# A PSUM free list, whole-row weight loads and one joined round in an attention + SwiGLU kernel

## The chip, the cores and the metric

The kernel runs on one core of one Trainium2 chip. The metric is the device time of one execution in microseconds (us). TensorE does matrix products into PSUM, which both kernels use as eight banks of 128 x 512 FP32 values; VectorE and ScalarE carry results out of PSUM; GpSimd issues the loads that cast to bf16; SyncE issues stores and DMA transposes.

## The reference, cut to what matters

```python
a = softmax(phi, axis=2)                    # over the 576 positions; 8 batches, 8 heads, 32 memories
k_m = einsum('bhsm,bhsd->bhmd', a, k)       # "K sums"
v_m = einsum('bhsm,bhsd->bhmd', a, v)       # "V sums"
attn = softmax(q @ k_m.T / sqrt(64), axis=-1)
x = (attn @ v_m) as rows of 512             # 4608 tokens
g, val = x @ w_gate, x @ w_val              # 512 -> 1536
out = (silu(g) * val) @ w_out               # 1536 -> 512
```

The kernel never forms `x`. For each batch it forms U = v_m @ W (a "U round", one per chunk of 512 columns of `w_gate` and `w_val`), and then the gates and values as `attn @ U`.

Of the kernel before, what the change touches and what calls it, by code (L numbers as in the profile page):

```python
# [14 lines left out]
def kernel(  # L15
# [39 lines left out]
    work = ctx.enter_context(tc.tile_pool(name="work", bufs=3))  # L55
    ps = ctx.enter_context(tc.tile_pool(name="ps", bufs=6, space=bass.MemoryType.PSUM))
    po = ctx.enter_context(tc.tile_pool(name="po", bufs=2, space=bass.MemoryType.PSUM))

# [5 lines left out]
    phis, kvs, qs, qTs = {}, {}, {}, {}  # L64
    box = {}
    Q_SLOT = (0, 1, 0, 0, 1, 0, 1, 0)

# [48 lines left out]

    def load_w(which, c, half):

        src = (moe_w_gate, moe_w_val)[which]
        if half == 0:  # L120
            W[which, c] = wpool.tile(
                [128, 2, NP, HC], BF16, tag=f"W{which}{c}", name=f"W{which}{c}"
            )
        f0 = c * CH + half * HC
        nc.gpsimd.dma_start(
            out=W[which, c][:, half],
            in_=src[:, f0:f0 + HC].rearrange("(i p) f -> p i f", p=128),
        )

    WO = {}  # L130
# [107 lines left out]
    def kv_T(b, parts):  # L238
        p = ps.tile([128, 3, 128], BF16, tag="b", name="p_T")
        if 0 in parts:  # L240
            kTs[b] = att.tile([128, 3, 128], BF16, tag="kT", name="t_kT")
        if 1 in parts:
            nc.tensor.transpose(p[:, 2], bvs.pop(b).rearrange("p g d -> p (g d)"), ident)
        if 0 in parts:
            bk = bks.pop(b)
            for g in range(NG):
                nc.tensor.transpose(p[:, g], bk[:, g].rearrange("p a d -> p (a d)"), ident)
        lo, hi = (0 if 0 in parts else 2), (3 if 1 in parts else 2)
        nc.vector.tensor_copy(out=kTs[b][:, lo:hi], in_=p[:, lo:hi])

    def kv_items(b, beside=None):


        def run_sums():
            o = NG * 2 * D
            p = ps.tile([128, o + NG], FP32, tag="b", name="p_kv")
            kv_denominators(b, p, o)
            kv_sum(b, p, (0, 1))
            kv_reciprocal(b, p, o)
            kvv = p[:, 0:o].rearrange("p (g w d) -> p g w d", g=NG, w=2)  # L260
            k_norm(b, kvv[:, :, 0:1, :])
            v_norm(b, kvv[:, :, 1, :])
            if beside:
                beside()

        return [run_sums, lambda: kv_T(b, (0, 1))]

    def k_items(b):


        def denominators():
            p = ps.tile([128, NG], FP32, tag="b", name="p_S")
            kv_denominators(b, p, 0)
            kv_reciprocal(b, p, 0)

        def sums():
            p = ps.tile([128, NG * D], FP32, tag="b", name="p_kv")
            kv_sum(b, p, (0,))
            k_norm(b, p.rearrange("p (g a d) -> p g a d", g=NG, a=1))

        return [denominators, sums, lambda: kv_T(b, (0,))]

    def v_direct(b):


        p = ps.tile([128, NP, M], FP32, tag="b", name="p_vT")
        for i in range(NP):
            for j in range(J):
                for g in range(NG):
                    nc.tensor.matmul(  # L290
                        p[64 * g:64 * g + 64, i],
                        lhsT=kvs[b][:, 1, 2 * i + g, j * D:(j + 1) * D],
                        rhs=ephis[b][:, j, g, i],
                        start=(j == 0),
                        stop=(j == J - 1),
                        tile_position=(0, 64 * g),
                    )
        nc.vector.tensor_copy(out=kTs[b][:, 2], in_=p.rearrange("p i m -> p (i m)"))
        scaled.add(b)

    def q_T(b, g, n, eng="v"):


        pq = ps.tile([128, 2, HALF], BF16, tag="b", name="p_q")
        for i in range(2):
# [13 lines left out]
        else:  # L319
            nc.vector.tensor_copy(out=t, in_=pq)  # L320

    def gv_banks():
        return [
            ps.tile([128, CH], FP32, tag="b", name=f"p_{'gv'[r]}") for r in range(2)
        ]

    def scores(b, g):
# [12 lines left out]
        for r in range(2):  # L340
            nc.scalar.activation(out=e[:, r], in_=p[r][:, 0:HALF], func=AF.Exp, scale=sm_scale)  # L341
        es[b, g] = e

    lzs = {}

    def z_inv(b, g):
# [3 lines left out]
        for r in range(2):  # L350
            nc.tensor.matmul(  # L351
                p[r][:, 0:HALF], lhsT=bones, rhs=es[b, g][:, r], start=True, stop=True
            )
            nc.scalar.activation(out=lz[:, r], in_=p[r][:, 0:HALF], func=AF.Ln)
        nc.scalar.activation(out=lz, in_=lz, func=AF.Exp, scale=-1.0)  # L355
        lzs[b, g] = lz
# [10 lines left out]

    def u_round(b, parts, evac, spare=-1):


        banks = []
        for n_part, (which, c, halves) in enumerate(parts):
            pool, tag = (po, "o") if n_part == spare else (ps, "b")
            w0, w1, h0, h1 = which[0], which[-1] + 1, halves[0], halves[-1] + 1
            n = (h1 - h0) * HC
            p = [
                pool.tile([128, 2, HC], FP32, tag=tag, name=f"p_u{g}").rearrange(
                    "p a f -> p (a f)"
                )
                for g in range(NG)  # L380
            ]
            for w in which:
                o = (w - w0) * n
                for i in range(NP):
                    for g in range(NG):
                        nc.tensor.matmul(  # L386
                            p[g][32 * i:32 * i + 32, o:o + n],
                            lhsT=kTs[b][64 * g:64 * g + 64, 2, 32 * i:32 * i + 32],
                            rhs=W[w, c][64 * g:64 * g + 64, h0:h1, i],
                            start=True,  # L390
# [3 lines left out]
            for g in range(NG):  # L394
# [6 lines left out]
                src = p[g][:, 0:(w1 - w0) * n].rearrange("p (a f) -> p a f", f=HC)  # L401
                banks.append((dst, src, rSs[b][:, g, 0] if b in scaled else None))
        for (t, p, r), e in zip(banks, evac):
            if e == "a":
# [6 lines left out]
            else:  # L411
                nc.vector.tensor_scalar(out=t, in0=p, scalar1=r, scalar2=None, op0=ALU.mult)


# [7 lines left out]
    def gv_half(b, s, which):  # L422

        jf, r = s // 2, s % 2
        c, o = jf // 4, jf % 4
        p = ps.tile([128, CH], FP32, tag="b", name=f"p_{'gv'[which]}")
        for g in range(NG):
# [6 lines left out]
            )  # L434
        return p[:, 0:HALF]

    def gv_gate(b, s):
# [5 lines left out]
        sg = work.tile([128, HALF], BF16, tag="sg", bufs=8, name="t_sg")  # L443
        nc.scalar.activation(out=sg, in_=gate, func=AF.Silu)  # L444
        col = (b % 2) * S + r * HALF
        dst = hts[b // 2, jf][:, col:col + HALF]

        def mul():
            val = gv_half(b, s, 1)
            nc.vector.tensor_tensor(out=dst, in0=sg, in1=val, op=ALU.mult)  # L450

# [26 lines left out]
    def out_units(c, u, eng):  # L478
# [3 lines left out]
        def unit(jf):  # L482
            def run():
                if jf == 0:
                    mine["p"] = po.tile([128, DM], FP32, tag="o", name="p_oo")
                nc.tensor.matmul(  # L486
# [6 lines left out]
                if jf == NJF - 1:  # L493
# [3 lines left out]
                    else:  # L497
                        nc.vector.tensor_copy(out=t_o, in_=mine["p"])  # L498
                    for (r0, m, bb, jj, pp) in token_segments(2 * c * S + 128 * u, 128):
                        nc.sync.dma_start(  # L500
# [7 lines left out]
    def out_units_end(c, u):  # L508
# [4 lines left out]
        def unit(half, jf):  # L513
            def run():
                if jf == 0:
                    mine["p"] = po.tile([128, h], FP32, tag="o", name="p_oo")
                nc.tensor.matmul(  # L517
# [6 lines left out]
                if jf == NJF - 1:  # L524
                    t_o = work.tile([128, h], FP32, tag="to", name="t_o")
                    nc.scalar.copy(out=t_o, in_=mine["p"])
                    segs = token_segments(2 * c * S + 128 * u, 128)
                    for n, (r0, m, bb, jj, pp) in enumerate(segs):
# [23 lines left out]

    def u_item(b, c, evac="avav", spare=-1):

        return lambda: u_round(b, (((0,), c, (0, 1)), ((1,), c, (0, 1))), evac, spare)

    def u_half(b, which, c, half, evac, spare=-1):

        return lambda: u_round(b, ((which, c, (half,)),), evac, spare)

# [26 lines left out]
    def warm(n):  # L587

        p = po.tile([128, DM], FP32, tag="o", name="p_oo")
        for _ in range(n):  # L590
            nc.tensor.matmul(p[:, 0:128], lhsT=bones, rhs=bones, start=True, stop=True)  # L591


# [17 lines left out]
    load_v(1)  # L611
    for c in range(NCH):
        for half in range(2):
            for which in range(2):
                load_w(which, c, half)
    load_wo(0)
# [51 lines left out]
    for s in range(4):  # L668
        gv_gate(0, s)
    run([u_half(0, (1,), 0, 0, "va"), u_half(1, (1,), 0, 0, "va", 0)])  # L670
    for s in range(2):
        gv_gate(1, s)
    flush_mul(3)
    run([u_half(0, (0, 1), 0, 1, "va", 0)])
    flush_mul(2)
    run(g1[2:4])
    run([u_half(1, (0, 1), 0, 1, "av", 0)] + g0[4:8] + g1[4:5])
    for c in range(1, NCH):
        s = 8 * c
        run([u_item(0, c, spare=1)] + g1[s - 3:s] + g0[s:s + 5])  # L680
        run([u_item(1, c, spare=1)] + g0[s + 5:s + 8] + g1[s:s + 5])
    run(g1[-3:])
# [101 lines left out]
```

## The kernel before: the parts that the change touches

PSUM comes from two pools: six banks rotate through everything, two are kept for output sums, for a short burst of "warm-up" products, and as a spare for some U rounds.

```python
ps = tile_pool(name="ps", bufs=6, space=PSUM)
po = tile_pool(name="po", bufs=2, space=PSUM)
...
def warm(n):                               # keeps TensorE busy until data comes
    p = po.tile([128, DM], FP32, tag="o", name="p_oo")
    for _ in range(n):
        nc.tensor.matmul(p[:, 0:128], lhsT=bones, rhs=bones, start=True, stop=True)
...
for c in range(NCH):                       # three chunks, two halves, gate and value
    for half in range(2):
        for which in range(2):
            load_w(which, c, half)         # 128 x 4 x 256, cast to bf16 by GpSimd's queue
...
run([u_half(0, (0, 1), 0, 1, "va", 0)])    # U round: batch 0, second half of chunk 0
flush_mul(2)
run(g1[2:4])                               # two gate/value slots of batch 1
run([u_half(1, (0, 1), 0, 1, "av", 0)] + g0[4:8] + g1[4:5])
for c in range(1, NCH):                    # chunks 1 and 2 of batches 0 and 1
    s = 8 * c
    run([u_item(0, c, spare=1)] + g1[s - 3:s] + g0[s:s + 5])
    run([u_item(1, c, spare=1)] + g0[s + 5:s + 8] + g1[s:s + 5])
```

A slot is one gate (two products of 288 columns, then SiLU on ScalarE) and one value (two products, then a multiplication on VectorE). In the trace these are `p_g`, `p_v`, `t_sg` and `t_h`; a U round is `p_u` into `t_U`; output sums are `p_oo`. From batch 2 on, slots are mixed with output products of the batches before, and one U round and the K/V sums of the next batch lie in between.

The softmax here doesn't subtract the row's maximum and nothing guards it: scores larger than these inputs give would overflow.

## Time and profile before

| | before |
|---|---|
| median of the timed runs | 249.0 us (248.97 to 249.04) |
| span in the profile | 247.4 us |
| first gate starts | 27.98 us |
| last matmul starts | 243.32 us, 215.34 us after the first gate |

Read it from TensorE: its busy share is 97%, but a share hides short holes. I measured holes as the distance between two starts less the pace of a steady stream (216 ns for 512 columns, 122 ns for 288). The lines are in the prediction; there the columns of a timeline row are start, duration, engine, line, operation, tiles and count, and in brackets an idle time with what ended it.

### The profile page before, as it was taken

Reading aid. Unit: us, or ns where it says so; the run is one execution under the profiler, and the core shown is the slowest. Engines: PE = TensorE matmul, PEld = TensorE weight load, DVE = VectorE, ACT = ScalarE, POOL = GpSimd, SP = SyncE. Lnnn points to the kernel's source line nnn. Section 1 sums busy time; section 2 is a strip of 40 time slices with the busy share of each in tenths; the row PEclk is TensorE's granted clock in tenths of the full one; section 3 lists DMA queues with packets and bytes.
Section 4 is the critical chain, followed back from the end, with each engine's and each line's share of the span. In section 5 each row is a group of like instructions: output and inputs, shape, how many; then the busy total and the mean of one; then the engine's idle time right before and its main releaser. Section 6 shows DMA issues by size and latency. Waiting matters only on the chain.

```text
span 247.4 us, 6614 instructions
## 1 busy us (share of the span) xinstructions
PE 239.5 (97%) x2600; PEld 150.7 (61%) x2600; DVE 158.5 (64%) x337; ACT 165.0 (67%) x356; POOL 54.5 (22%) x85
## 2 busy tenths in 40 slices
PE   7998899999999999999999999999999999999993
PEld 7966567774544765467645665476646655467543
DVE  0146499993437688479847778478846876587420
ACT  2467789885087568966896677966895677676201
POOL 8342455000060004070505240090007000000000
PEclk9999999999999999999999999999999999999999
DMA  7999999999689986997897599589414411310143
GB/s 183 205 203 203 196 198 200 233 197 199 126 160 244 236 186 89 212 283 139 122 239 204 90 119 235 166 119 197 91 48 116 72 42 42 87 42 0 45 128 85
DMA packets 49167, 37.00 MB, mean 150 GB/s; under 512 B 15984, under 2 KB 43888, under 8 KB 49136
## 3 DMA queue, kind: packets, MB, share of 16 engines
q0 software_dynamic: 27632, 22.42, 57.5%
q1 hardware_dynamic: 20496, 13.37, 22.9%
q10 hardware_dynamic: 1008, 0.79, 1.2%
q8 instruction: 20, 0.33, 0.5%
q14 instruction: 11, 0.09, 0.1%
HBM read 42.47 MB, written 9.44 MB: 210 GB/s over the span
## 4 chain that ended last, share of the span: by engine, by line
PE 75%; DMA 20%; POOL 3%; issue 1%; ACT 0%; POOLq 0%
PE p_oo L486 32%; PE p_g L428 17%; PE p_v L428 17%; DMA t_kv<-in_v_dram 14%; PE p_u L386 4%; DMA W<-in_moe_w_val_dram 4%; DMA t_qT<-t_q 2%; PE p_kv L183 2%; PE p_oo L517 1%; POOL t_q L93 1%; POOL t_kv L81 1%; PE p_g L351 0%; PE p_v L351 0%; PE p_g L331 0%; POOL t_q L100 0%
## 5 line engine op out<-in xcount | busy, mean ns | idle before, releaser
L486 PE MATMUL p_oo<-WO,t_h 128*128 128x512 bf16 x420 | 108.6, 379 | 0.0
L444 ACT ACTIVATE t_sg<-p_g 128x288 bf16<-128x288 f32 x192 | 76.6, 413 | 31.3 <-PE p_g L428 24.2
L450 DVE TENSOR_TENSOR t_h<-t_sg,p_v 128x288 bf16<-128x288 bf16 x192 | 83.9, 453 | 18.0 <-PE p_v L428 14.1
L428 PEld LDWEIGHTS <-t_U 128*128 128x128 bf16 x768 | 74.2, 98 | 30.7 <-issue 2.5
L428 PE MATMUL p_g<-t_A,t_U 128*128 128x288 bf16 x384 | 77.5, 286 | 0.0
L428 PE MATMUL p_v<-t_A,t_U 128*128 128x288 bf16 x384 | 76.9, 286 | 0.0
L486 PEld LDWEIGHTS <-t_h 128*128 128x128 bf16 x420 | 39.5, 98 | 41.1 <-issue 6.0
L498 DVE COPY t_o<-p_oo 128x512 f32<-128x512 f32 x27 | 18.6, 691 | 32.1 <-PE p_oo L486 29.4
L410 DVE CAST t_U<-p_u 128x512 bf16<-128x512 f32 x42 | 26.7, 684 | 6.8 <-PE p_u L386 6.8
L406 ACT CAST t_U<-p_u 128x512 bf16<-128x512 f32 x30 | 15.8, 592 | 9.0 <-PE p_u L386 9.0
L496 ACT COPY t_o<-p_oo 128x512 f32<-128x512 f32 x8 | 4.7, 588 | 20.5 <-PE p_oo L486 10.6
L100 POOL DMA_DIRECT2D t_q<-in_q_dram x6 | 4.7, 782 | 60.6 <-DMA t_qT<-t_q 59.8
L591 PE MATMUL p_oo<-bones 128*128 128x128 bf16 x198 | 14.6, 234 | 1.5 <-DVE bones L606 1.5
L386 PE MATMUL p_u<-W,t_kT 64*32 64x512 bf16 (+1 forms) x416 | 15.6, 365 | 0.5 <-DMA W<-in_moe_w_val_dram 0.3
L153 ACT ACTIVATE t_ephi<-t_phi 96x768 bf16<-96x768 f32 x16 | 12.5, 843 | 4.3 <-DMA t_phi<-in_phi_dram 4.2
L591 PEld LDWEIGHTS <-bones 128*128 128x128 bf16 x198 | 12.8, 106 | 2.2 <-DVE bones L606 1.5
L166 POOL COPY t_mark<-t_A 1x1 bf16<-1x1 bf16 x4 | 0.7, 182 | 53.9 <-DVE t_A L360 53.9
L360 DVE TENSOR_TENSOR t_A<-t_E,t_lz 128x576 bf16<-128x576 bf16 x16 | 11.5, 750 | 0.3 <-ACT t_lz L355 0.3
L355 ACT ACTIVATE t_lz<-t_lz 128x576 f32<-128x576 f32 x16 | 10.9, 684 | 0.5
L341 ACT ACTIVATE t_E<-p_g 128x288 bf16<-128x288 f32 x16 | 6.6, 412 | 6.9 <-PE p_v L331 6.3
L170 POOL TENSOR_TENSOR t_es<-t_es,t_ephi 96x256 f32<-96x256 f32 x16 | 10.7, 668 | 1.3
L408 ACT ACTIVATE t_U<-p_u,t_rS 128x512 bf16<-128x512 f32 (+1 forms) x14 | 8.3, 628 | 2.9 <-PE p_u L386 2.9
(58 smaller groups left out, 164.1 us busy)
## 6 DMA issues: line engine op xcount, KB each, us to landing
t_kv<-in_k_dram POOLq DMA_DIRECT2D x8, 576.0 KB, 9.8
t_kv<-in_v_dram POOLq DMA_DIRECT2D x8, 576.0 KB, 14.5
out_dram<-t_o SPq DMA_DIRECT2D x23, 192.0 KB, 2.5
t_phi<-in_phi_dram POOLq DMA_DIRECT2D x6, 576.0 KB, 15.2
t_q<-in_q_dram POOLq DMA_DIRECT2D x6, 576.0 KB, 7.4
out_dram<-t_o SPq DMA_DIRECT2D x24, 128.0 KB, 2.4
W<-in_moe_w_gate_dram POOLq DMA_DIRECT2D x6, 256.0 KB, 13.2
W<-in_moe_w_val_dram POOLq DMA_DIRECT2D x6, 256.0 KB, 12.2
```

The lines of the kernel that those rows point to most:

```text
L153: nc.scalar.activation(out=t[:, :, g].rearrange("p j i m -> p i j m"), in_=src[:, g], func=AF.Exp)
L355: nc.scalar.activation(out=lz, in_=lz, func=AF.Exp, scale=-1.0)
L360: nc.vector.tensor_tensor(out=a, in0=es.pop((b, g)), in1=lzs.pop((b, g)), op=ALU.mult)
L386: nc.tensor.matmul(p[g][32 * i:32 * i + 32, o:o + n], lhsT=kTs[b][64 * g:64 * g + 64, 2, 32 * i:32 * i + 32], rhs=W[w, c][64 * g:64 * g + ...
L406: nc.scalar.copy(out=t, in_=p)
L410: nc.vector.tensor_copy(out=t, in_=p)
L428: nc.tensor.matmul(p[:, 0:HALF], lhsT=Us[b, c, g][:, o // 2, which, 128 * (o % 2):128 * (o % 2 + 1)], rhs=atts[b, g][:, r], start=(g == 0) ...
L444: nc.scalar.activation(out=sg, in_=gate, func=AF.Silu)
L450: nc.vector.tensor_tensor(out=dst, in0=sg, in1=val, op=ALU.mult)
L486: nc.tensor.matmul(mine["p"], lhsT=hts[c, jf][:, 128 * u:128 * (u + 1)], rhs=WO[jf], start=(jf == 0), stop=(jf == NJF - 1),)
L498: nc.vector.tensor_copy(out=t_o, in_=mine["p"])
L591: nc.tensor.matmul(p[:, 0:128], lhsT=bones, rhs=bones, start=True, stop=True)
```

## The change

Its intent: let a bank be taken as soon as it is free, whoever used it; move the weights in fewer and longer pieces; save two switches of TensorE between tile sizes. The core of the diff, with cuts:

```diff
-    ps = ctx.enter_context(tc.tile_pool(name="ps", bufs=6, space=bass.MemoryType.PSUM))
-    po = ctx.enter_context(tc.tile_pool(name="po", bufs=2, space=bass.MemoryType.PSUM))
+    ps = ctx.enter_context(tc.tile_pool(name="ps", bufs=1, space=bass.MemoryType.PSUM))
+    free = [f"B{n}" for n in range(8)]
+    held = {}
+    def bank(shape, dtype, name):
+        tag = free.pop(0)
+        t = ps.tile(shape, dtype, tag=tag, name=name)
+        held[id(t)] = tag, t
+        return t
+    def done(*tiles):
+        for t in tiles:
+            free.append(held.pop(id(t))[0])
 ...   (every ps.tile and po.tile becomes bank(...), with done(...) after its last reader)
     def warm(n):
-        p = po.tile([128, DM], FP32, tag="o", name="p_oo")
+        p = bank([128, DM], FP32, "p_warm")
         for _ in range(n):
             nc.tensor.matmul(p[:, 0:128], lhsT=bones, rhs=bones, start=True, stop=True)
+        free.insert(0, held.pop(id(p))[0])
 ...
+    for c in range(1, NCH):
+        for which in range(2):
+            load_w(which, c)               # 128 x 4 x 512
 ...
-    run([u_half(0, (0, 1), 0, 1, "va", 0)])
+    run([u_half(0, (0, 1), 0, 1, "va"), u_half(1, (0, 1), 0, 1, "av")])
     flush_mul(2)
-    run(g1[2:4])
-    run([u_half(1, (0, 1), 0, 1, "av", 0)] + g0[4:8] + g1[4:5])
+    run(g1[2:4] + g0[4:8] + g1[4:5])
```

More of the change, by code (lines that the diff above doesn't have):

```diff
@@ L115, with load_w, w_part @@
     HC = CH // 2
-    def load_w(which, c, half):
+    def load_w(which, c, half=None):
         src = (moe_w_gate, moe_w_val)[which]
-        if half == 0:
+        split = half is not None
+        if not half:
             W[which, c] = wpool.tile(
-                [128, 2, NP, HC], BF16, tag=f"W{which}{c}", name=f"W{which}{c}"
+                [128, 2, NP, HC] if split else [128, NP, CH], BF16,
+                tag=f"W{which}{c}", name=f"W{which}{c}",
             )
-        f0 = c * CH + half * HC
+        f0, n = (half * HC, HC) if split else (0, CH)
         nc.gpsimd.dma_start(
-            out=W[which, c][:, half],
-            in_=src[:, f0:f0 + HC].rearrange("(i p) f -> p i f", p=128),
-        )
+            out=W[which, c][:, half] if split else W[which, c],
+            in_=src[:, c * CH + f0:c * CH + f0 + n].rearrange("(i p) f -> p i f", p=128),
+        )
+    def w_part(which, c, i, g, halves):
+        w = W[which, c][64 * g:64 * g + 64]
+        h0, h1 = halves[0], halves[-1] + 1
+        return w[:, h0:h1, i] if c == 0 else w[:, i, HC * h0:HC * h1]
     WO = {}
@@ L238, in kv_T @@
     def kv_T(b, parts):
-        p = ps.tile([128, 3, 128], BF16, tag="b", name="p_T")
+        p = bank([128, 3, 128], BF16, "p_T")
         if 0 in parts:
@@ L249, in kv_T @@
         nc.vector.tensor_copy(out=kTs[b][:, lo:hi], in_=p[:, lo:hi])
+        done(p)
     def kv_items(b, beside=None):
@@ L255, in run_sums @@
             o = NG * 2 * D
-            p = ps.tile([128, o + NG], FP32, tag="b", name="p_kv")
+            p = bank([128, o + NG], FP32, "p_kv")
             kv_denominators(b, p, o)
@@ L262, in run_sums @@
             v_norm(b, kvv[:, :, 1, :])
+            done(p)
             if beside:
@@ L271, in denominators @@
         def denominators():
-            p = ps.tile([128, NG], FP32, tag="b", name="p_S")
+            p = bank([128, NG], FP32, "p_S")
             kv_denominators(b, p, 0)
             kv_reciprocal(b, p, 0)
+            done(p)
         def sums():
-            p = ps.tile([128, NG * D], FP32, tag="b", name="p_kv")
+            p = bank([128, NG * D], FP32, "p_kv")
             kv_sum(b, p, (0,))
             k_norm(b, p.rearrange("p (g a d) -> p g a d", g=NG, a=1))
+            done(p)
         return [denominators, sums, lambda: kv_T(b, (0,))]
     def v_direct(b):
-        p = ps.tile([128, NP, M], FP32, tag="b", name="p_vT")
+        p = bank([128, NP, M], FP32, "p_vT")
         for i in range(NP):
@@ L298, in v_direct @@
         nc.vector.tensor_copy(out=kTs[b][:, 2], in_=p.rearrange("p i m -> p (i m)"))
+        done(p)
         scaled.add(b)
     def q_T(b, g, n, eng="v"):
-        pq = ps.tile([128, 2, HALF], BF16, tag="b", name="p_q")
+        pq = bank([128, 2, HALF], BF16, "p_q")
         for i in range(2):
@@ L320, in q_T @@
             nc.vector.tensor_copy(out=t, in_=pq)
+        done(pq)
     def gv_banks():
-        return [
-            ps.tile([128, CH], FP32, tag="b", name=f"p_{'gv'[r]}") for r in range(2)
-        ]
+        return [bank([128, CH], FP32, f"p_{'gv'[r]}") for r in range(2)]
     def scores(b, g):
@@ L341, in scores @@
             nc.scalar.activation(out=e[:, r], in_=p[r][:, 0:HALF], func=AF.Exp, scale=sm_scale)
+        done(*p)
         es[b, g] = e
@@ L354, in z_inv @@
             nc.scalar.activation(out=lz[:, r], in_=p[r][:, 0:HALF], func=AF.Ln)
+        done(*p)
         nc.scalar.activation(out=lz, in_=lz, func=AF.Exp, scale=-1.0)
@@ L366, with u_round @@
     scaled = set()
-    def u_round(b, parts, evac, spare=-1):
+    def u_round(b, parts, evac):
         banks = []
-        for n_part, (which, c, halves) in enumerate(parts):
-            pool, tag = (po, "o") if n_part == spare else (ps, "b")
+        for which, c, halves in parts:
             w0, w1, h0, h1 = which[0], which[-1] + 1, halves[0], halves[-1] + 1
             n = (h1 - h0) * HC
-            p = [
-                pool.tile([128, 2, HC], FP32, tag=tag, name=f"p_u{g}").rearrange(
-                    "p a f -> p (a f)"
-                )
-                for g in range(NG)
-            ]
+            p = [bank([128, CH], FP32, f"p_u{g}") for g in range(NG)]
             for w in which:
@@ L388, in u_round @@
                             lhsT=kTs[b][64 * g:64 * g + 64, 2, 32 * i:32 * i + 32],
-                            rhs=W[w, c][64 * g:64 * g + 64, h0:h1, i],
+                            rhs=w_part(w, c, i, g, halves),
                             start=True,
@@ L401, in u_round @@
                 src = p[g][:, 0:(w1 - w0) * n].rearrange("p (a f) -> p a f", f=HC)
-                banks.append((dst, src, rSs[b][:, g, 0] if b in scaled else None))
-        for (t, p, r), e in zip(banks, evac):
+                banks.append((dst, src, p[g], rSs[b][:, g, 0] if b in scaled else None))
+        for (t, p, home, r), e in zip(banks, evac):
             if e == "a":
@@ L412, in u_round @@
                 nc.vector.tensor_scalar(out=t, in0=p, scalar1=r, scalar2=None, op0=ALU.mult)
+            done(home)
     hts = {}
@@ L425, in gv_half @@
         c, o = jf // 4, jf % 4
-        p = ps.tile([128, CH], FP32, tag="b", name=f"p_{'gv'[which]}")
+        p = bank([128, CH], FP32, f"p_{'gv'[which]}")
         for g in range(NG):
@@ L434, in gv_half @@
             )
-        return p[:, 0:HALF]
+        return p
     def gv_gate(b, s):
@@ L443, in gv_gate @@
         sg = work.tile([128, HALF], BF16, tag="sg", bufs=8, name="t_sg")
-        nc.scalar.activation(out=sg, in_=gate, func=AF.Silu)
+        nc.scalar.activation(out=sg, in_=gate[:, 0:HALF], func=AF.Silu)
+        done(gate)
         col = (b % 2) * S + r * HALF
@@ L449, in mul @@
             val = gv_half(b, s, 1)
-            nc.vector.tensor_tensor(out=dst, in0=sg, in1=val, op=ALU.mult)
+            nc.vector.tensor_tensor(out=dst, in0=sg, in1=val[:, 0:HALF], op=ALU.mult)
+            done(val)
         pend.append(mul)
@@ L484, in run @@
                 if jf == 0:
-                    mine["p"] = po.tile([128, DM], FP32, tag="o", name="p_oo")
+                    mine["p"] = bank([128, DM], FP32, "p_oo")
                 nc.tensor.matmul(
@@ L498, in run @@
                         nc.vector.tensor_copy(out=t_o, in_=mine["p"])
+                    done(mine["p"])
                     for (r0, m, bb, jj, pp) in token_segments(2 * c * S + 128 * u, 128):
@@ L515, in run @@
                 if jf == 0:
-                    mine["p"] = po.tile([128, h], FP32, tag="o", name="p_oo")
+                    mine["p"] = bank([128, h], FP32, "p_oo")
                 nc.tensor.matmul(
@@ L526, in run @@
                     nc.scalar.copy(out=t_o, in_=mine["p"])
+                    done(mine["p"])
                     segs = token_segments(2 * c * S + 128 * u, 128)
@@ L551, in q_items, with u_item, u_half @@
         ]
-    def u_item(b, c, evac="avav", spare=-1):
-        return lambda: u_round(b, (((0,), c, (0, 1)), ((1,), c, (0, 1))), evac, spare)
-    def u_half(b, which, c, half, evac, spare=-1):
-        return lambda: u_round(b, ((which, c, (half,)),), evac, spare)
+    def u_item(b, c, evac="avav"):
+        return lambda: u_round(b, (((0,), c, (0, 1)), ((1,), c, (0, 1))), evac)
+    def u_half(b, which, c, half, evac):
+        return lambda: u_round(b, ((which, c, (half,)),), evac)
     def u_three(b):
@@ L611 @@
     load_v(1)
-    for c in range(NCH):
-        for half in range(2):
-            for which in range(2):
-                load_w(which, c, half)
+    for half in range(2):
+        for which in range(2):
+            load_w(which, 0, half)
+    for c in range(1, NCH):
+        for which in range(2):
+            load_w(which, c)
     load_wo(0)
@@ L669 @@
         gv_gate(0, s)
-    run([u_half(0, (1,), 0, 0, "va"), u_half(1, (1,), 0, 0, "va", 0)])
+    run([u_half(0, (1,), 0, 0, "va"), u_half(1, (1,), 0, 0, "va")])
     for s in range(2):
@@ L673 @@
     flush_mul(3)
-    run([u_half(0, (0, 1), 0, 1, "va", 0)])
+    run([u_half(0, (0, 1), 0, 1, "va"), u_half(1, (0, 1), 0, 1, "av")])
     flush_mul(2)
-    run(g1[2:4])
-    run([u_half(1, (0, 1), 0, 1, "av", 0)] + g0[4:8] + g1[4:5])
+    run(g1[2:4] + g0[4:8] + g1[4:5])
     for c in range(1, NCH):
         s = 8 * c
-        run([u_item(0, c, spare=1)] + g1[s - 3:s] + g0[s:s + 5])
-        run([u_item(1, c, spare=1)] + g0[s + 5:s + 8] + g1[s:s + 5])
+        run([u_item(0, c)] + g1[s - 3:s] + g0[s:s + 5])
+        run([u_item(1, c)] + g0[s + 5:s + 8] + g1[s:s + 5])
     run(g1[-3:])
```

## The prediction

> **What bounds the kernel now.** I read first the page's busy shares, then the waits of TensorE, then the TensorE timeline around each wait, and last the chain that ended last. The page:
>
> ```profile
> span 247.4 us, 6614 instructions
> PE 239.5 (97%) x2600; PEld 150.7 (61%) x2600; DVE 158.5 (64%) x337; ACT 165.0 (67%) x356; POOL 54.5 (22%) x85
> L486 PE MATMUL p_oo<-WO,t_h 128*128 128x512 bf16 x420 | 108.6, 379 | 0.0
> L428 PE MATMUL p_g<-t_A,t_U 128*128 128x288 bf16 x384 | 77.5, 286 | 0.0
> ```
>
> A busy share of 97% does not by itself say that TensorE works at its full rate, so I used distances between starts. In the chain, 28 output matmuls take 6.04 us, which is 216 ns each; in the timeline one pair of 288-column matmuls follows the last by 0.245 us, 122 ns each. Both are the pace of a stream with no hole. From 56 us to the end I found only one hole beyond that pace and the mode changes. So the span can shrink only where TensorE has holes, and those lie before 86 us. Four matter. The waits of TensorE:
>
> ```profile
> PE p_vT L290 <- DMA t_kv<-in_v_dram: 0.9, 1, 0.9
> PE p_u L386 <- DMA W<-in_moe_w_val_dram: 0.3, 1, 0.3
> PE p_u L386 <- DMA W<-in_moe_w_gate_dram: 0.2, 1, 0.2
> ```
>
> The first and third (25.6 and 27.1 us) wait for the last V tile and for the first half of weight chunk 0, and the change leaves both loads as they are. The second is chunk 1 of the value weights; then a small repeated hole, then one for K and V of batch 3 (TensorE timeline, three windows):
>
> ```profile
> 35.36 0.41 PE L428 MATMUL p_v<-t_A,t_U 128*128 128x288 bf16 x2
> 35.70 0.41 PE L386 MATMUL p_u<-W,t_kT 64*32 64x512 bf16 x8
> 36.39 0.41 PE L386 MATMUL p_u<-W,t_kT 64*32 64x512 bf16 x8 [0.29 <-DMA W<-in_moe_w_val_dram]
> ...
> 42.55 0.41 PE L428 MATMUL p_v<-t_A,t_U 128*128 128x288 bf16 x2
> 42.85 0.41 PE L428 MATMUL p_g<-t_A,t_U 128*128 128x288 bf16 x2
> 43.15 0.41 PE L428 MATMUL p_v<-t_A,t_U 128*128 128x288 bf16 x2
> ...
> 85.27 0.44 PE L203 MATMUL p_kv<-ones,t_ephi 96*128 96x1 bf16 x12
> 85.78 0.85 PE L183 MATMUL p_kv<-t_kv,t_ephi 96*32 96x128 bf16 x48
> ```
>
> The value half of the round could start at 35.70 + 0.24 = 35.94 and starts at 36.39: a hole of 0.45 us (the view shows 0.29 because it counts modelled ends). At 42.85 and 43.15 a pair comes after 0.30 instead of 0.245 us: 0.11 us a round, three rounds, 0.33 us. At 85.78 the K/V sums start 0.14 us later than the twelve tiny matmuls before them and the usual 0.09 us change would let them. The chain of waits says why:
>
> ```profile
> 25.86 10.40 DMA W<-in_moe_w_val_dram
> ...
> 63.16 4.98 DMA t_qT<-t_q
> ...
> 70.25 15.49 DMA t_kv<-in_v_dram
> 85.78 0.85 PE p_kv L183 x48
> ```
>
> V of batch 3 lands at 85.74, behind a DMA transpose (63.16 to 68.13) that waited for Q of batch 2, the last of the first 28 GpSimd loads (landed at 63.06). That is one unbroken transfer chain from the start of the kernel.
>
> **What the Trainium skill says.** "Perfetto Trace Analysis", section Matmul Optimizations, advises that all 8 PSUM banks be used; here 6 rotate among everything and 2 are kept for outputs, and the trace shows what that costs: 0.33 us. "DMA: Bandwidth & Descriptors", section Why small descriptors are slow (HBM only), names a fixed cost per packet. The trace agrees in kind only: a 512-byte packet takes 60 ns and a 1024-byte one 98 ns, but what the queue moves hardly changes, as the next view shows. "TensorEngine Tiling (Array Packing)", section Key Properties, says that changing the tiling mode drains TensorE; the trace shows 94 ns on entry to a U round (64x32 tiles) and 92 ns on exit, beyond the pace.
>
> ```profile
> 27.00:39.00 12.00, 11.59 (x155) 7.55 (x156) 9.93 (x23) 10.25 (x25) 6.82 (x9) 1.00 1.45 197
> 41.70:47.00 5.30, 5.30 (x56) 3.66 (x54) 5.19 (x12) 4.73 (x12) 0.78 (x1) 1.00 1.29 204
> ```
>
> The last column is GB/s: 197 while half-chunk weights stream (512-byte packets), 204 while output weights (1024-byte) and K do.
>
> **The change part by part.**
>
> *Whole rows.* Eight GpSimd loads of 256 KB become four of 512 KB, with the same bytes in the same order behind the same loads. Before, landings of 256 KB follow each other by 1.33 us (26.95 to 41.61 us in 11 steps), so 512 KB take 2.67; an output-weight load of 512 KB takes 2.59 or 2.60 (41.61 to 44.20, 47.14 to 49.74). That is 0.07 us a load, 0.14 us for the two of chunk 1 and 0.28 us for all four. The window rates give 2.1 MB x (1/197 - 1/204 GB/s) = 0.37 us; I take 0.30. So chunk 1 lands at about 36.1 instead of 36.26, and everything queued behind chunk 2, Q of batch 2 and so V of batch 3 included, lands about 0.3 us earlier. Four issues fewer at 0.74 us each on GpSimd save nothing: the transfers are queued ahead without a gap.
>
> *Joined rounds.* The instruction lists show 2600 matmuls in both kernels. One exit and one entry go away: 92 + 94 = 0.19 us at 32.8 us. But TensorE then meets the wait for chunk 1 at 36.39, and simply waits 0.19 us longer. On the path: nothing.
>
> *Eight banks in order of release.* In the stretch from 36.4 to 56 us VectorE is as full as TensorE: from one evacuation of U at 41.31 to the next at 46.00, 4.69 us, it never rests, while TensorE needs 4.58 (eight slots of 0.49 and a round of 0.65). TensorE is held at the seventh bank it asks for after a round, at 42.85, because with six rotating banks that is the one of the first new gate, whose SiLU ends just then. With eight in a row, the seventh and eighth are those of the round's second half, free at about 42.5 and 42.7, earlier than asked for (42.79 and 43.04). The lag that VectorE builds up is 0.11 us a round over four rounds, about what the two extra banks hold. So most of the 0.33 us goes: say 0.30.
>
> *Sum.* TensorE gets to 85 us earlier by 0.14 (chunk 1) + 0.30 (banks) = 0.44 us. V of batch 3 comes earlier by 0.3 only. The K/V sums start at the later of the two: before, they started 0.14 us after TensorE was ready, so the gain there is the smaller of 0.44 + 0.14 and 0.3, that is **0.3 us**. The hole at 85.78 grows from 0.14 to about 0.28 us. After it TensorE has no hole, and nothing of the change reaches the rest. 248.98 - 0.3 = **248.7 us**, 0.1%.
>
> **The rivals.**
>
> *The transfer chain gives nothing.* A row piece of 2 KB is read at a pitch of 6 KB, while output weights are read without a gap; the higher rate may belong to those. 512-byte packets already move 197 of 204 GB/s, which speaks for this. Then V lands when it did, and the time is 248.9 to 249.0 although TensorE saved 0.3 us earlier.
>
> *The transfer chain gives more,* for instance because the four larger loads are queued earlier. Against it: the queue had no gap to fill. Then TensorE binds: 0.44 + 0.14 = 0.58 us, 248.4.
>
> *A new wait for a bank.* Outputs, which hold a bank for twelve matmuls, now stand in the same line as gates and values, so a late output copy (ScalarE's waits 9.7 us for a store near 69 us) could hold up a gate. Against it: at most one or two output banks are held, so six or seven remain for the rest, and TensorE had no hole there with six. I allow it 0.3 us of loss: 249.0 to 249.3.
>
> *VectorE stays the bound at 40 to 56 us.* More banks let TensorE run ahead but make VectorE no faster. That matters only if the four rounds outlast the extra banks; even so the result at 85.78 is set by V, and the time would stay at 248.7.
>
> **Range and chances.** Three runs of the kernel before lie within 0.07 us. The sum of the holes that the change can touch is 0.45 + 0.33 + 0.14 + 0.19, about 1.1 us, the most that it could give, and the losses I can name are some 0.3 us. The range is 248.1 to 249.2, with the centre at 248.7. Two per cent would be 5 us: no part has that size, so both outer chances are 0.01.
>
> **What would show it.** Right: no pair after 0.30 us at 42 to 53 us; the last of the chunk-1 weights landing near 36.1; one U round fewer with 64x256 matmuls, and the hole before 36.4 grown to about 0.5 us; V of batch 3 landing near 85.4 and TensorE waiting for it about 0.3 us; from there on the same rows shifted by one constant. Wrong: pairs still 0.30 us apart (the banks were not the cause), V landing at 85.7 (rows do not help), a new wait of TensorE on a copy after 56 us (the single list hurts), or a landing that moves by more than 0.5 us.

## The result, and the profile after

The changed kernel takes 248.6 us in the median of four runs: 248.39, 248.42, 248.78, and one of 252.27; the three fast runs alone have a median of 248.42. Executions over 1.5% slower than the fastest of the same kernel are left out of the means. The kernel before takes 249.0. The ratio of the fast runs is 0.9981, a gain of 0.47 us, with a 95% interval of 0.9961 to 1.0001, so the times alone do not quite exclude that nothing was gained. (A ratio is the mean time of one kernel's fast runs over that of the other's in the same rounds, so not quite the ratio of the medians.) The page of the changed kernel, its busy shares and the shares by engine of the chain that ended last:

```profile
span 246.6 us, 6607 instructions
PE 239.5 (97%) x2600; PEld 151.2 (61%) x2600; DVE 157.9 (64%) x337; ACT 164.5 (67%) x356; POOL 51.4 (21%) x81
...
PE 95%; DVE 1%; ACT 1%; issue 0%
```

The last line is the news. In the kernel before it read:

```profile
PE 75%; DMA 20%; POOL 3%; issue 1%; ACT 0%; POOLq 0%
```

So transfers left the chain altogether, and TensorE now binds from its first instruction. The three windows of TensorE that the prediction showed, in the changed kernel:

```profile
35.54 0.41 PE L452 MATMUL p_v<-t_A,t_U 128*128 128x288 bf16 x2
35.88 0.63 PE L409 MATMUL p_u<-W,t_kT 64*32 64x512 bf16 x16
36.43 0.42 PE L452 MATMUL p_g<-t_A,t_U 128*128 128x288 bf16 x2
...
42.49 0.41 PE L452 MATMUL p_g<-t_A,t_U 128*128 128x288 bf16 x2
42.74 0.41 PE L452 MATMUL p_v<-t_A,t_U 128*128 128x288 bf16 x2
42.98 0.41 PE L452 MATMUL p_g<-t_A,t_U 128*128 128x288 bf16 x2
...
84.65 0.44 PE L226 MATMUL p_kv<-ones,t_ephi 96*128 96x1 bf16 x12
85.03 0.85 PE L206 MATMUL p_kv<-t_kv,t_ephi 96*32 96x128 bf16 x48
```

All three holes are gone: the round on chunk 1 runs in one piece, the pairs follow each other by 0.245 us, and the K/V sums start 0.38 us after the tiny matmuls, where the kernel before needed 0.51. From there on every row is 0.75 us earlier. (Chunk 1 landed at 35.81 us, just before TensorE came for it at 35.88.) But the start of TensorE is not earlier, it is later. Before and after:

```profile
25.62 0.94 PE L290 MATMUL p_vT<-t_ephi,t_kv 96*64 96x32 bf16 x48 [0.90 <-DMA t_kv<-in_v_dram]
26.49 0.40 PE L591 MATMUL p_oo<-bones 128*128 128x128 bf16 x4
27.08 0.41 PE L386 MATMUL p_u<-W,t_kT 64*32 64x256 bf16 x16 [0.20 <-DMA W<-in_moe_w_gate_dram]
```

```profile
25.98 0.94 PE L317 MATMUL p_vT<-t_ephi,t_kv 96*64 96x32 bf16 x48
26.85 0.40 PE L619 MATMUL p_warm<-bones 128*128 128x128 bf16 x4
27.30 0.41 PE L409 MATMUL p_u<-W,t_kT 64*32 64x256 bf16 x16
```

Before, TensorE stood here 0.9 us waiting for V of batch 1: the start had slack. After, no transfer is named, and the work comes 0.2 to 0.4 us later. The delay is older: the last long warm-up, of 24 products, begins at 24.41 us instead of 23.21, 1.20 us later. Of this, 0.54 us are there when the first warm-up ends (the last of its 130 products starts at 10.83 us instead of 10.29; e4 below says why). The other 0.66 us are lost between 11 and 24 us, where matmuls that follow a warm-up come late: by 0.22 us beyond the pace at 11.10, 13.92 and 19.20 us, where the kernel before has no hole. The first of these, before and after:

```profile
1.52 8.99 PE L591 MATMUL p_oo<-bones 128*128 128x128 bf16 x130 [1.52 <-DVE bones L606]
10.34 0.44 PE L203 MATMUL p_S<-ones,t_ephi 96*128 96x1 bf16 x12
```

```profile
1.52 9.53 PE L619 MATMUL p_warm<-bones 128*128 128x128 bf16 x130 [1.52 <-DVE bones L635]
11.10 0.44 PE L226 MATMUL p_S<-ones,t_ephi 96*128 96x1 bf16 x12
```

The matmuls at 25.98, 27.30 and 28.21 us (the first gate) come 0.22 us late as well, but there the warm-up is only part of the cause, as e5 will show.

### The profile page after: what moved, and what is told of

Same layout as the page of the kernel before. It is cut to its first block, busy times and chain, and to the rows that moved or that the text cites. A ratio compares the mean times of both kernels' runs of the same rounds, so it can differ in the third digit from the quotient of the medians.

```text
span 246.6 us, 6607 instructions
## 1 busy us (share of the span) xinstructions
PE 239.5 (97%) x2600; PEld 151.2 (61%) x2600; DVE 157.9 (64%) x337; ACT 164.5 (67%) x356; POOL 51.4 (21%) x81
## 4 chain that ended last, share of the span: by engine, by line
PE 95%; DVE 1%; ACT 1%; issue 0%
PE p_oo L512 38%; PE p_g L452 19%; PE p_v L452 19%; PE p_u L409 5%; PE p_warm L619 5%; PE p_kv L206 2%; PE p_oo L544 1%; DVE t_qT L348 1%; PE p_g L379 1%; PE p_g L358 1%; PE p_v L379 1%; PE p_vT L317 1%; ACT t_E L368 1%; PE p_T L270 0%; PE p_kv L226 0%
## 5 line engine op out<-in xcount | busy, mean ns | idle before, releaser
L619 PE MATMUL p_warm<-bones 128*128 128x128 bf16 x198 | 15.2, 239 | 1.5 <-DVE bones L635 1.5
L619 PEld LDWEIGHTS <-bones 128*128 128x128 bf16 x198 | 13.4, 109 | 2.2 <-DVE bones L635 1.5
## 6 DMA issues: line engine op xcount, KB each, us to landing
t_phi<-in_phi_dram POOLq DMA_DIRECT2D x6, 576.0 KB, 16.5
```

## The experiments

Every experiment gave correct results. The table collects what their traces show, in us; it is worked out from starts of matmuls and completions of loads. "Hole 1" is the one in the round on chunk 1, "hole 2" the one before the K/V sums of batch 3, "0.05s" counts pairs that come some 0.05 us late between 38 and 53 us, "W stream" is the time from the last landing of chunk 0 to the last of chunk 2, and "rest" is from the first gate to the last matmul.

| kernel | first gate | hole 1 | 0.05s | V of batch 3 lands | hole 2 | rest | W stream |
|---|---|---|---|---|---|---|---|
| before | 27.98 | 0.46 | 6 | 85.74 | 0.14 | 215.34 | 10.70 |
| changed | 28.21 | 0 | 0 | 84.94 | 0 | 214.35 | 10.21 |
| e1 rows alone | 27.78 | 0.13 | 6 | 85.45 | 0.38 | 215.25 | 10.26 |
| e2 banks alone | 28.30 | 0.06 | 0 | 85.68 | 0.50 | 214.97 | 10.75 |
| e3 join alone | 27.86 | 0 | 8 | 85.79 | 0 | 215.55 | (late start) |
| e4 changed, again | 28.80 | 0 | 0 | 83.78 | 0 | 214.36 | 10.16 |
| e5 warm-up bank to the back | 27.89 | 0.09 | 0 | 84.97 | 0.17 | 214.66 | 10.19 |
| e9 banks, hole 2 opened | 27.97 | 0.33 | 0 | 85.81 | 0 | 214.75 | 10.70 |
| e10 e5, hole 2 opened | 27.81 | 0.15 | 0 | 85.39 | 0 | 214.55 | 10.23 |
| e11 e5 without the join | 28.06 | 0.13 | 0 | 84.75 | 0 | 214.56 | 10.17 |

**The theory** is the prediction's: gates in series. TensorE must pass the landing of chunk 1, then the pace of VectorE, then the landing of V of batch 3, and what it saves ahead of a gate that opens later is lost at that gate. (The second of these gates did not hold up; see "Eight banks" in the next section.) **The rivals**: only the banks matter (B), or every part gives back its own hole, whatever the others do (C).

### The three parts alone, and the whole once more

e1: the loads, and the access to them, of the changed kernel in the old pools.

```diff
-for c in range(NCH): for half ...: for which ...: load_w(which, c, half)
+for half ...: for which ...: load_w(which, 0, half)
+for c in range(1, NCH): for which ...: load_w(which, c)
```

> Only the whole-row loads of weight chunks 1 and 2, in the old pools and with the old rounds. Theory A (gates in series: TensorE meets the landing of chunk 1 at 36 us, then the pace of VectorE at 42 to 53 us, then the landing of V of batch 3 at 85.7 us, and only the last gate to open counts): chunk 1 lands about 0.4 us earlier, V of batch 3 0.3 to 0.8 us earlier, the three 0.30 us spacings stay, and the kernel gains 0.4 to 0.6 us (248.4 to 248.6). Rival B (the rows move no bytes faster, the gain of the change is that of the banks): 0.0 to 0.1 us. Rival C (holes add up, each part gives its own hole back): 0.45 us.

Measured: 248.64 us (248.46 to 248.86) against 248.89 for the kernel before in the same rounds, ratio 0.9992 (0.9980 to 1.0004). The profile shows the theory at work: the first gate came 0.20 us sooner and hole 1 shrank from 0.46 to 0.13, so TensorE came to the K/V sums 0.53 us sooner, and there hole 2 grew from 0.14 to 0.38, because V of batch 3 came only 0.29 us earlier in that run. The later of the two counts: 0.29 us. The expected 0.4 to 0.6 us was too much. The interval of the times holds B and C too, so this reading rests on the profile.

e2: the single list alone.

```diff
-    load_w(which, c) / the joined round
+    load_w(which, c, half) / the two rounds of the kernel before
```

> Only the single list of eight banks, half-row loads and separate rounds as before. Theory A: the 0.30 us spacings go (0.33 us of TensorE time), but V of batch 3 still lands at 85.7 us, so the hole before the K/V sums grows from 0.14 to about 0.45 us and the kernel gains 0.14 us at most. Rival B: it gains the 0.4 us of the whole change. Rival C: 0.33 us. A new wait of TensorE on its own warm-up matmuls (0.2 us each, the warm-up bank goes back to the front of the list) should be seen before 28 us, hidden behind the landing of V of batch 1.

Measured: 249.08 us (248.82 to 249.12), ratio 1.0004 (0.9992 to 1.0017). Rival B falls, and so does C: the late pairs are all gone, 0.33 us are saved by 56 us, and nothing is left at the end. TensorE at the K/V sums, with the wait in brackets:

```profile
84.86 0.44 PE L218 MATMUL p_kv<-ones,t_ephi 96*128 96x1 bf16 x12
85.73 0.85 PE L198 MATMUL p_kv<-t_kv,t_ephi 96*32 96x128 bf16 x48 [0.43 <-DMA t_kv<-in_v_dram]
```

What TensorE saved it spent here. The first gate was also late, 28.30 us.

e3: the joined round alone.

```diff
-run([u_half(0, (0, 1), 0, 1, "va", 0)])
+run([u_half(0, (0, 1), 0, 1, "va", 0), u_half(1, (0, 1), 0, 1, "av", -1)])
```

> Only the joined rounds, in the old pools and with half-row loads. Theory A and B: 0.0 us, since the wait for chunk 1 at 36.4 us grows by the 0.19 us saved (0.45 to 0.64 us). Rival C: 0.19 us.

Measured: 248.98 us (248.76 to 249.23), ratio 1.0003 (0.9991 to 1.0015). No gain is seen, but this is weak evidence: the interval just holds rival C's 0.19 us, and the profile does not show the theory's mechanism. In that run the last piece of chunk 0 landed at 31.52 us, 0.6 us later than in the others, so the wait came in the joined round itself (0.67 us) and not at chunk 1. The edit also moves the round of batch 1 from the spare banks to the rotating six, and there are eight late pairs instead of six.

e4: the changed kernel unaltered.

> The whole change again, as a control beside the three parts on the same chip. All theories: 248.3 to 248.8, 0.2 to 0.7 us under the kernel before. If the single runs fall into two groups, the clock of TensorE should be granted later in one of them (5.96 us in the profile, against 4.82 us in that of the kernel before).

Measured: 248.53 us (248.09 to 249.74), ratio 0.9992 (0.9975 to 1.0009). The rest after the first gate is 214.36 us, as in the first profile (214.35), but the first gate came at 28.80. So in these two profiles the time of the changed kernel is its first gate plus a constant. V of batch 3 had landed at 83.78, nearly 2 us before it was asked for. What moved the first gate? The rows below are one window from 4.80 to 7.40 us, the second column being TensorE with the count of its matmuls, for the changed kernel and then for e4:

```profile
4.80:7.40 2.60, 2.60 (x39) 2.60 (x38) 0.00 (x0) 0.71 (x1) 2.60 (x5) 1.00 1.20 246
```

```profile
4.80:7.40 2.60, 2.60 (x28) 2.60 (x27) 0.00 (x0) 0.74 (x1) 2.60 (x5) 1.00 1.20 243
```

The warm-up starts at 1.52 us in each, but runs at half pace (107 ns a product) until the full clock is granted: at 5.96 us in the first and at 7.21 in the second. (The 1.00 for the clock in these rows misleads: the trace's record of the clock begins only with the grant. The distances between starts show it, 107 ns before and 56 after.) With a fixed number of warm-up products, a late grant moves all that follows. The Trainium skill, "TensorE: Matmul & The Clock Gate", section Part 1: The HAM clock gate (the "warmup" mystery), puts this at around 4 us of sustained work, varying with the phase of a free-running window; the runs here agree in kind, but spread wider, from 2.7 to 5.9 us.

### Why the start is late, and whether hole 2 can be opened

The instruction lists say what a warm-up does in the changed kernel. `free.insert(0, ...)` puts its bank at the front of the list, so the next real matmul takes the same bank and waits for TensorE's own last product in it. The list of waits of the changed kernel has one of these that is long enough to be listed:

```profile
PE p_T L270 <- PE p_warm L619: 0.2, 1, 0.2
```

e5 puts the bank at the back.

```diff
-        free.insert(0, held.pop(id(p))[0])
+        done(p)
```

> The changed kernel, but the warm-up bank goes to the back of the list, so that no real matmul follows the warm-up in its own bank. Theory A (the changed kernel is now bound from its first gate on, and its first gate comes late, at 28.2 us and 28.8 us in two profiles, because each warm-up makes the next matmul wait 0.2 us for the end of the last one in the same bank): the holes of 0.22 us at 26, 27.3 and 28.2 us go, the first gate comes at 27.8 to 28.2 us, and the kernel gains 0.2 to 0.4 us on the changed one, until V of batch 3 (84 to 85.5 us) takes over. Rival D (the late gate is chance alone, the grant of the clock): no holes less, no gain.

Measured: **248.37 us** (248.27 to 248.54) against 249.2 for the kernel before, ratio 0.9969 (0.9957 to 0.9981), clear of 1. The start of TensorE in its profile:

```profile
25.80 0.94 PE L317 MATMUL p_vT<-t_ephi,t_kv 96*64 96x32 bf16 x48 [0.18 <-DMA t_kv<-in_v_dram]
26.67 0.40 PE L619 MATMUL p_warm<-bones 128*128 128x128 bf16 x4
26.99 0.43 PE L409 MATMUL p_u<-W,t_kT 64*32 64x256 bf16 x16
```

TensorE waits for V again, so the slack is back. The holes of 0.22 us at the places of 11.10, 13.92 and 19.20 us are gone. The expectation named three others, and of these it is right only in part: where the changed kernel has 0.22 us at 27.30 and 28.21 us, e5 still has 0.09 (the change of tile size) and 0.19. The first gate comes at 27.89 us although this run had the latest grant of all, 7.38 us. The profiled first gates with the bank at the front and a grant at 5.28, 5.72, 5.96, 6.00 and 7.21 us are 27.97, 28.17, 28.21, 28.30 and 28.80: they follow the grant. The kernels without it stay between 27.69 and 28.06 whatever the grant (4.21 to 7.38). So rival D (chance alone) falls: the grant is chance, but only the front-of-list waits let it through to the end. The gain of 0.2 to 0.4 us on the changed kernel is not shown: the two were not timed in the same rounds, and their intervals overlap. What is shown is that e5 is faster than the kernel before, which neither session of the changed kernel shows clear of 1. Hole 2 is back, 0.17 us, as the theory wants of an earlier TensorE.

e6, e7 and e8 were to open hole 2 by placing the K/V sums of batch 3 two slots later.

```diff
-(kv_items(3, ...), 10, 14),
+(kv_items(3, ...), 12, 16),
```

> The same, with the K/V sums of batch 3 placed two slots later (some 1.4 us), so that V of batch 3 has landed when TensorE comes. Theory A: no hole before these sums in any run, and the time follows the first gate alone: the last matmul starts 214.3 us after it; 247.9 to 248.4. Rival D: as the run before it.

> The kernel before with only the K/V sums of batch 3 placed two slots later. Theory A: the hole of 0.14 us goes and the kernel gains 0.1 us, no more, since chunk 1 and the three spacings of 0.30 us stay. Rival E (V of batch 3 binds more than the one profile shows): 0.4 us or more.

> The single bank list alone with the K/V sums of batch 3 placed two slots later. Theory A: what the banks alone saved before 56 us (0.4 us) and lost again at 85.7 us now comes through: 0.3 to 0.5 us under the kernel before, 248.4 to 248.6, where the bank list alone gave 0.0. Rival B (the banks give nothing that counts): 0.1 us, as for the kernel before with the same move.

Measured: e6 248.22 us in the profiled run but 250.66 and 254.89 to 257.23 in the others; e7 248.75, 248.92 and 251.82 in fast runs, 252.96 to 256.55 in slow ones; e8 251.04 (250.68 to 252.76). These three are a failed edit. Two output stores come with the K/V sums, so these moved too, and the DMA transpose of Q of batch 3 slipped ahead of them in SyncE's queue. The chain of waits of e8:

```profile
80.58 17.13 DMA t_qT<-t_q
...
99.82 13.96 DMA t_kv<-in_v_dram
113.83 0.85 PE p_kv L198 x48
```

At its usual place (90.46 us) the transpose took some 5 us; here, in the middle of other transfers, it took 17. The loads of batch 4 wait for it, and TensorE stood 1.5 us for V of batch 4, besides 0.7 us at 97.6 us for a SiLU. The transpose took 16.5 and 16.4 us in the profiled runs of e6 and e7 too, but there V of batch 4 landed in time (110.71 and 111.37 us, against 113.78 in e8) and nothing was lost.

e9 and e10 repeat e8 and e6 with the transpose moved along, so that SyncE's order is as before.

```diff
-(kv_items(3, ...), 10, 14),   ([lambda: load_qT(3)], 12, 12),
+(kv_items(3, ...), 12, 16),   ([lambda: load_qT(3)], 14, 14),
```

> The single bank list alone with the K/V sums of batch 3 two slots later, as e8, but with the DMA transpose of Q of batch 3 moved along, so that it keeps its place behind two output stores (in e8 it slipped ahead of them, ran 17 us among the loads of batches 4 and 5 and made V of batch 4 late by 7 us: a fault of the edit, not a verdict). Theory A (gates in series): the transpose takes its old place, no hole at 86 or 113 us, the banks' 0.4 us come through: 248.4 to 248.7, 0.2 to 0.5 us under the kernel before. Rival B (the banks give nothing that counts): 0.0 to 0.1 us.

The 7 us in this text are a slip: V of batch 4 landed at 113.78 us in e8 and at 111.11 in the kernel before, 2.7 us later.

Measured: 248.54 us (248.52 to 249.01) against 248.95, ratio 0.9989 (0.9975 to 1.0002). The banks alone gave 1.0004 with hole 2 shut and give 0.4 us in the medians with it open. The interval still touches 1, so the times support the theory without proving it; the profile shows it more plainly: no hole 2, V at 85.81 and the K/V sums at 86.38, and a rest of 214.75 us, 0.59 less than before. But only 0.33 of these are the pairs: 0.14 are hole 2 itself, which the move alone might open, and 0.13 are hole 1, which was smaller in this run. The control, the kernel before with this clean move, was not run. Hole 1, which the banks cannot touch, is there:

```profile
35.68 0.41 PE L401 MATMUL p_u<-W,t_kT 64*32 64x512 bf16 x8
36.25 0.41 PE L401 MATMUL p_u<-W,t_kT 64*32 64x512 bf16 x8 [0.16 <-DMA W<-in_moe_w_val_dram]
```

> The changed kernel with the warm-up bank at the back of the list (as e5) and the K/V sums of batch 3 two slots later with the transpose moved along (as e9). Theory A: no hole of the K/V sums at 85 us, the last matmul starts 214.2 to 214.4 us after the first gate (27.8 us): 248.1 to 248.3, as fast as e5 (248.37) or up to 0.2 us faster.

Measured: 248.28 us (248.15 to 248.67), ratio 0.9975 (0.9962 to 0.9987). With hole 2 open, what is left is hole 1 again (0.15 us): chunk 1 now binds a TensorE that starts on time. It is not shown to be faster than e5.

e11 takes the join out of e5.

```diff
-run([u_half(0, (0, 1), 0, 1, "va"), u_half(1, (0, 1), 0, 1, "av")])
+run([u_half(0, (0, 1), 0, 1, "va")])      # and the round of batch 1 after g1[2:4]
```

> As e5 (warm-up bank at the back), but with the two half-chunk rounds apart again: rows and banks without the join. Theory A: the wait for chunk 1 (0.04 us in e5) is no longer there to take up the saved 0.19 us, but the four evacuations in a row that the join brings make holes of 0.03 + 0.04 + 0.12 us right behind it; so the join is worth 0.0 to 0.05 us: 248.3 to 248.5. Rival C (each part gives its own hole back): 0.19 us slower than e5, 248.55.

Measured: 248.32 us (248.18 to 248.47), ratio 0.9974 (0.9962 to 0.9987), beside 248.28 for e10 on the same chip, which has the join and no hole 2. The join is worth nothing that can be seen. The spread of the times is too wide to exclude rival C's 0.19 us, but the rest after the first gate is 214.55 us with the join and 214.56 without, so it is not there in the profiles. Where the join is, three holes of 0.03, 0.04 and 0.12 us follow it at 32 to 34 us, 0.19 us together; in e11 they are absent.

e12 shortens the first warm-up of e10.

```diff
-    warm(130)
+    warm(110)
```

> As e10 with 110 warm-up matmuls ahead of the first sums instead of 130. Theory A: the landings of V of batch 1 and of the first weights (25.6 and 26.8 us) set the first gate at 27.8 us whether the warm-up ends at 10 or at 11 us, now that the waits in the same bank are gone: no gain on e10 (0.0 to 0.1 us). Rival F (the start of TensorE is still what binds): 0.5 us or more, the first gate at 27.3 us.

Measured: 249.19 us (248.5 to 249.38), ratio 1.0006 (0.9993 to 1.0019): slower than e10 by 0.9 us. The first gate in its profile is at 27.91 us, so rival F falls, but a loss was not expected either. The profiled run is the fastest of the five (248.5) and shows only one new hole of 0.21 us, at 78.5 us, where the normalised attention of batch 2 comes late. What the other four runs lost stays open.

## Why the prediction was right, point by point

**The time** was right: 248.7 predicted, 248.6 measured, inside the range. Part of that is luck. The range of 248.1 to 249.2 also holds the 249.0 of the kernel before. The fast runs gained 0.47 us rather than 0.3. And two misses cancel in part: V and TensorE gained more than predicted (0.80 and 0.98 us), and the start lost 0.23 us that the prediction did not expect.

**The signs** that it named came out mixed. The late pairs are gone, one U round of 64x256 matmuls is gone, and the later rows are shifted by one constant, as it said. But the hole before 36.4 us vanished instead of growing to 0.5 us, and TensorE did not wait for V of batch 3. One of its own signs of being wrong came true: the landing of V moved by 0.80 us, more than 0.5.

**Whole rows: right in kind, too small.** The step said 0.07 us a load and "I take 0.30" for all four. The W stream went from 10.70 to 10.21 us, 0.49 us, and between 10.16 and 10.26 in the other kernels with whole rows against 10.70 and 10.75 without. In the window from 27 to 39 us, which the prediction showed at 197 GB/s, the changed kernel moves:

```profile
27.00:39.00 12.00, 11.89 (x161) 7.89 (x160) 10.21 (x25) 10.29 (x27) 4.62 (x6) 1.00 1.28 205
```

Q of batch 2 landed 0.98 us earlier and V of batch 3 0.80 us. That landing varies from run to run, from 83.8 to 85.5 us in the eight profiles with whole rows (mean 84.8) and from 84.9 to 86.1 in the six without (mean 85.7). So the mis-sized term is the gain of the transfer chain: 0.3 predicted, about 0.9 measured. Only 0.49 of it are in the weight stream; where the rest arises was not traced.

**Joined rounds: right in effect, not in the reason.** "On the path: nothing." e3 and e11 show no gain. In the changed kernel the reason is another: the wait for chunk 1 that was to swallow the 0.19 us is gone, and the holes behind four evacuations in a row swallow them instead.

**Eight banks: right in effect, wrong on VectorE.** No late pair is left in any kernel with the list, as predicted for 42.79 and 43.04 us. But the step "The lag that VectorE builds up is 0.11 us a round over four rounds" failed: no lag builds up. In both kernels VectorE starts its multiplication 0.93 us after the second value product right behind a U round, and 0.39 us after it, the least that occurs, from the fifth or sixth slot on. In the changed kernel a round takes 4.58 us (its U rounds stand at 40.53, 45.11 and 49.69 us in the chain), the pace that the prediction gave TensorE, and VectorE still catches up in each. So VectorE's throughput did not bound this stretch; with six banks TensorE came back to a bank that the SiLU or the multiplication, held up behind the copies of U, had not yet emptied. Whether eight banks in plain rotation would have done as well as the list ordered by release was not tested.

**The sum: the rule held, the verdict failed.** "The K/V sums start at the later of the two" is what e1, e2 and e9 show. But the step that said V of batch 3 would be the later one, with hole 2 at 0.28 us, failed in the changed kernel: there is none. V came earlier than thought, and TensorE later than thought. The rival "the transfer chain gives more" (TensorE binds, 248.4) is what the profile shows.

**What the prediction missed** is the cost of the list at the start. It looked for a new bank wait among outputs, and found none there rightly; the wait is on the warm-up, behind which the list hands out the same bank. Its waits used up the slack before V of batch 1, so that the late grant of the clock came through: the first gate was 0.23 us later in the profile and 0.8 in e4. From the first gate to the K/V sums TensorE saved 0.98 us (57.80 before, 56.82 after): 0.46 (hole 1) + 0.33 (pairs) + 0.14 (hole 2) make 0.93, and the join adds 0.19 and its holes take 0.19; 0.05 are not accounted for. Of the 0.98, 0.23 were given back at the start, which leaves the 0.75 us of the profile.

## What to carry to other kernels

A saving on the busiest engine counts only up to the next transfer that it waits for; look for the next gate before adding up holes, and undo parts one by one, because parts that are worth nothing alone can be worth something behind an opened gate (here the banks: the profile of e9 shows it, its times do not prove it). A free list ordered by release is good for banks that other engines must empty, but a bank that TensorE itself has just written belongs at the back, else the next matmul waits for that product to end (0.22 us here); with that one line changed, the kernel was clear of the one before (248.37 us, ratio 0.9969). When an edit moves work, check the order in every DMA queue as well: a transpose that slipped past two stores took 17 us instead of 5, and in e8 that cost 2 us.

## What the Trainium skill lacked or had wrong

- No page that I read gives the cost of a matmul that waits for the last one in the same PSUM bank: 0.22 us beyond the pace at 11.10, 13.92 and 19.20 us in the changed kernel, and none at the same places in e5.
- "DMA: Bandwidth & Descriptors", section Why small descriptors are slow (HBM only), has no rate for casting loads by row length: doubling the pieces from 512 to 1024 bytes as written cut the W stream from 10.70 to 10.21 us (196 to 205 GB/s for 2.1 MB).
- "TensorE: Matmul & The Clock Gate", section Part 1: The HAM clock gate (the "warmup" mystery), gives about 4 us with a spread of 0.5 us from run to run: here the grant came 2.7 us (e12) to 5.9 us (e5) after the first matmul.
- The same DMA page does not tell what a DMA transpose costs beside loads: 16.4 to 17.1 us in e6, e7 and e8, against 5.08 us for the same transpose in the kernel before.
